# Batched loads for the low halves of w1, a later softmax and an earlier weight request at the change of block size, in a fused convolution and mixture-of-experts kernel

## The chip, the cores and the metric

The kernel runs on one core of one Trainium2 chip. The core has a matrix engine (PE, whose weight loads are listed as PEld), a vector engine (DVE), a scalar engine (ACT), GpSimd (POOL) and SyncE (SP), which here does nothing but issue DMAs. Each engine works through its own list of instructions in order; they wait for one another by semaphores. The metric is the device time in microseconds (us) of one execution; less is better.

## The reference

For 8 sequences of 2880 tokens with 192 features, a causal convolution over 7 tokens is computed with its own softmax weights per token and head (8 heads of 24 features). Its output goes through a mixture of experts: of 4 groups the token takes the best, of that group's 4 experts the best, and its output is the expert's two-layer network times both softmax weights.

```python
w = np.exp(weight_gen - np.max(weight_gen, axis=-1, keepdims=True))
w = w / (np.sum(w, axis=-1, keepdims=True) + 1e-09)
x_unf = x_pad[:, idx, :].reshape(B, S, K, H, group)        # K = 7 taps, 8 heads of 24
x = np.einsum('bshk,bskhg->bshg', w, x_unf).reshape(B * S, D)   # 23040 x 192
g_idx = np.argmax(x @ w_group, axis=1)                     # 4 groups
...
    e_idx = np.argmax(xg @ w_expert[g], axis=1)            # 4 experts in each
    ...
        h = np.maximum(xg[mask_e] @ w1[g, e], 0.0)         # w1: 192 x 1024
        ye = h @ w2[g, e]                                  # w2: 1024 x 192
        out[tok_idx] = combined[:, None] * ye
```

## The kernel before

**Two halves that run side by side.** The *front* takes the tokens in 15 groups of 12 x 128 tokens, two chunks of six to a group. Per group it loads the weights `wt` and the tokens `xin` (`load_group`, L123 and L133), makes the softmax on DVE and ACT (`softmax`: maximum m L269, subtraction L271, exponential on ACT L272, sum z L277 to L281, product L283), forms the seven products per chunk on DVE (L298) and adds them there (L316) or, in the first groups, on PE (L339), computes the routing logits on PE (L379, with the one-hot counts L463) and the choice of expert on DVE (L350 to L493), and lets POOL scatter the tokens by expert into the DRAM table `rows` (L507). A new order of blocks is made whenever a *round* of groups is routed; groups 0 and 1 are the first round, each later one a round of its own.

The *MoE* takes the scattered tokens in blocks. Blocks 0 to 9, those of the first round, are *plain*: one unit of 128 rows, float32 weights as loaded (`wa`, 96x1024 twice), first product `ph` L934, its activation `hh` on ACT, second product `py` L972, output `y` L981. From block 10 on a block has two units of 128 rows and is *split*: its weights `wa` and its tokens are taken apart into a rounded part and a remainder (casts L843 and L852 on ACT, subtraction `wa<-raw,wa` L867 on DVE; tokens `xh` L914 on ACT, `xl` L867 on DVE). For these blocks the remainders of w1's last 64 rows are prepared once, in DRAM, by `halves`.

**halves.** For eight pairs of experts it loads a 128x1024 tile (`fetch`, two DMAs of 64x1024 on SP, L629; the page's DMA part has 256 KB for each), and in `lower_half` casts it with the sign turned (ACT, L621), stores the tile to `w1lo` (SP, L623) and adds the cast one onto it by an accumulating DMA (POOL, L624). The tiles are borrowed from `wa`, `wc` and `raw` buffers, which blocks 0 and on then use.

**What sets the order.** The program's order is made by hand. `front` is a generator that yields after each few instructions, and `blocks` fills it in between the MoE's units by a model of the engines' clocks (`clk`); `Until(t)` holds a generator back until DVE's model clock is t. `side` holds a softmax of the next group, which `beside` advances behind each product of the running group (n counts these steps, 14 to a group). The order that results is then kept on PE, ACT, DVE and SP. Weights are asked for (`ask`, kind 1 and 2 for w1, 3 for w2, 0 for tokens `xb`) by `ask_w` at the last unit of a block, and their DMAs go to SP's list in that order: tables L814, plain w1 L817, split w1 L819 and L826, w2 L830, `xb` L802.

Of the kernel before, what the change touches and what calls it, by code (L numbers as in the profile page):

```python
# [23 lines left out]
AHEAD = (1.0, 1.0, 2.5)  # L24
HURRY = 12
SPACED = range(2, 15)
HALVES = (36.0, 42.0, 48.0, 54.0, 60.0, 66.0, 72.0, 78.0)
WHOLE = 12
SINGLE = tuple((k,) for k in range(7))
MIXED = ((0, 1), (2,), (3,), (4,), (5,), (6,))  # L30
# [12 lines left out]
def conv_moe_kernel(ctx: ExitStack, tc: tile.TileContext, x, wgen, w_group, w_expert, w1, w2, out):  # L43
# [28 lines left out]
    ENDS = [r[0] for r in ROUNDS]  # L72
# [6 lines left out]
    FIRST = ENDS[0]  # L79
# [153 lines left out]
    state = {"slots": False, "open": False, "unit": 0, "starve": False, "ph": 0, "hold": False}  # L233
# [12 lines left out]
    def run(eng, cost, *deps):  # L246
        clk[eng] = max([clk[eng]] + [d + HOP for d in deps]) + cost
        return clk[eng]
# [360 lines left out]
    def halves():  # L609
        spare = wp.tile([P, 3, F], F32, name="wa", bufs=3)  # L610
        raws = [spare[:, k, :] for k in range(3)]
        raws.append(wp.tile([P, NFT, D], F32, name="wc", bufs=4).rearrange("p f d -> p (f d)")[:, 0:F])
        raws += [new_raw[k]() for k in range(2) for _ in range(2)]
        other = wp.tile([P, 3, F], F32, name="wa", bufs=3)
        his = [other[:, k, :] for k in range(3)] + [new_raw[2]()[:, 0:F]]
        his += [wp.tile([P, NFT, D], F32, name="wc", bufs=4).rearrange("p f d -> p (f d)")[:, 0:F] for _ in range(3)]
        his = [t.bitcast(F32R) for t in his]

        def lower_half(k):
            e, hi, raw = 2 * k, his[k % len(his)], raws[k]  # L620
            nc.scalar.activation(out=hi, in_=raw, func=AF.Copy, scale=-1.0)  # L621
            low = w1lo[e:e + 2].rearrange("e p f -> (e p) f")
            nc.sync.dma_start(out=low, in_=raw)  # L623
            nc.gpsimd.dma_start(out=low, in_=hi.bitcast(F32), accum_op=ALU.add)  # L624
            run("pool", 1.1, run("act", 1.0))

        def fetch(k):
            for h in range(2):
                nc.sync.dma_start(out=raws[k][h * HP:(h + 1) * HP, :], in_=w1v[2 * k + h, P:D, :])  # L629

        yield NEXT
        for k, raw in enumerate(raws):
            yield Until(HALVES[k])
            fetch(k)
            if k == 0:
                continue
            lower_half(k - 1)
        yield Until(HALVES[-1] + 6.0)
        lower_half(len(raws) - 1)

    def set_up():
        nc.gpsimd.memset(tri, 1.0)
        nc.gpsimd.affine_select(out=tri, in_=tri, compare_op=ALU.is_gt, fill=0.0, base=0, pattern=[[1, P]], channel_multiplier=-1)
        nc.gpsimd.memset(wr, 0.0)
        wev = w_expert.rearrange("g d e -> d g e")
        for dst, r in ((wr[:, 0, :], slice(0, P)), (wr[0:HP, 1, :], slice(P, D)), (wr[HP:P, 2, :], slice(P, D))):
            nc.gpsimd.dma_start(out=dst[:, 0:G], in_=w_group[r, :])
            nc.gpsimd.dma_start(out=dst[:, G:NL].rearrange("p (g e) -> p g e", g=G), in_=wev[r])
        pad2 = padding()
        for h in range(2):  # L650
            nc.gpsimd.dma_start(out=rows[NROW + h * BK:NROW + (h + 1) * BK, :].rearrange("(p t) c -> p t c", t=2), in_=pad2)
# [4 lines left out]
    def front():  # L656
        side = []
        set_up()
        load_group(1)
        next(slow[0][0])  # L660
        yield from softmax(0, 0, SC)
        rest = softmax(0, SC)

        def pace(g):
            return 99 if g <= FIRST else HURRY if g < MAIN + 3 else 8 if g in ENDS else 2

        def beside(g, n):
            rush = g >= FIRST and not grp[FIRST - 1].routed
            if not rush:
                for q in list(slow):  # L670
                    yield from move(slow, q, 2)
            for q in side[:1]:
                if not rush:
                    yield from move(side, q, 3)
            yield from routing(g)

        def routing(g):
            if ranking:
                yield from move(ranking, ranking[0], pace(g))
            if scoring and (not ranking or g < FIRST):  # L680
                yield from move(scoring, scoring[0], pace(g) if scoring[0][2].chunks == 2 or g >= FIRST - 1 else 3)

        def settle(g):
            while not grp[g].routed:
                qs = ranking or scoring
                q = qs[0]
                yield from move(qs, q, 99)
                if qs and qs[0] is q and q[1] is not None:
                    yield Until(q[1][1]) if q[1][0] == "time" else NEXT

        for g in range(ENDS[-1]):
            o = grp[g]
            o.routed = False
            scoring.append([logits(g, o), None, o])
            for n, c in enumerate(conv(g, o)):
                yield c
                if g == 0 and n < 6:
                    for c in islice(rest, None if n == 5 else 1):
                        yield c
                if n == (2 if state["slots"] else 0) and 1 <= g < ENDS[-1] - 1:  # L700
                    load_group(g + 1)
                if n >= (12 if state["slots"] else 4) and not o.ahead and g + 1 < ENDS[-1] and g != FIRST - 1:
                    o.ahead = True
                    side.append([softmax(g + 1), None])
                yield from beside(g, n)
                if g == FIRST - 1 and n in (7, 8):
                    if n == 7:
                        soft = softmax(FIRST)
                    yield next(soft)
            if g == FIRST - 1:  # L710
                for n, c in enumerate(soft):
                    yield c
                    yield from beside(g, n)
            yield from finish_all(side)
            if g:
                yield from settle(g - 1)
        yield from settle(ENDS[-1] - 1)
# [61 lines left out]
    def plain(n):  # L779
        return order[n][1] == 1  # L780
# [235 lines left out]
    def blocks(n0, n1, paced):  # L1016
# [24 lines left out]
        def ask_w(n):  # L1041
            ask(n, 1)
            ask(n, 2)
# [66 lines left out]
        for i in range(len(units) + LAG):  # L1110
            if i < len(units):
                n, u = units[i]
                last = units_of(n) - 1
                gemm1(cur, u)
                queue.append((cur, u))
                nxt_at = i + last + 1 - u
                if nxt_at < len(units):
                    if u == 0:
                        pump(units[nxt_at][0])
                        nxt = block(nxt_at)  # L1120
                        prep_d(nxt)
                    if u == 1:
                        prep_x(nxt, 0)
                    if u == last // 2 + 1 and nxt.nt > 2:
                        prep_x(nxt, 2)
                if u == last and i + 1 < len(units):
                    cur = nxt
            asks = []
            if i >= LAG:
                b, u = queue.pop(0)  # L1130
                gemm2(b, u)
                if u == units_of(units[i - LAG][0]) - 1:
                    finish(b)
                    if i - LAG + 1 < len(units):
                        asks.append(units[i - LAG][0] + 3)
            if i < len(units):
                n, at = units[i]
                end = at == last
                if end and n + 3 < n1 and (plain(n + 3) or plain(n + 2)):
                    ask_w(n + 3)  # L1140
                    if not plain(n + 3):
                        ask_w(n + 4)
                did = 0
                for job in list(jobs):
                    m, part, h = job
                    if m > n + 2 or (part == 3 and (m > n + 1 or at < LAG)):
                        continue
                    must = end and m == n + 1
                    if not must and (did >= 1 or (m, part) in want or not ready(m)):
                        continue  # L1150
                    jobs.remove(job)
                    work_split(job)
                    did += 1
                state["unit"] += 1
            flush()
            if paced:
                fill(clk["pe"] + AHEAD[0 if cur.plain else 1 if cur.o.whole else 2])
            for a in asks:
                ask_x(a)
            pump()  # L1160
# [45 lines left out]
```

## Time and profile before

| What | us |
|---|---|
| Median of three runs | 1193.74 |
| The three runs | 1194.24, 1193.74, 1187.65 |
| The profiled execution, own time | 1189.24 |
| Its span in the trace | 1187.3 |
| PE busy | 1129.4 (95%) |
| DVE busy | 958.4 (81%) |
| ACT, POOL busy | 647.2 (55%), 580.5 (49%) |

The span runs from the first to the last instruction of the trace; 1.9 us of the execution's own time lie outside it. Busy shares are means over the span. A number in brackets at the end of a row of the timeline is how long the engine stood idle just before, and what ended it; PE's clock in the windows is a share of full speed, 2.4 GHz.

### The profile page before, as it was taken

The numbers are of one execution on the slowest core, as the hardware profiler recorded it, in microseconds if no ns is written. First come the engines' busy times: TensorE is split into PE (matmuls) and PEld (weight loads), VectorE is DVE, ScalarE is ACT, GpSimd is POOL, SyncE is SP. The second block draws the span as 40 slices with busy tenths as digits, with TensorE's granted clock in tenths as the row PEclk, the third lists the DMA queues.
The fourth block names the chain that finished last, engine by engine and source line by source line (L and its number), as shares of the span: only waits on it lengthen the run. The fifth ranks groups of instructions, "written<-read, shape, count | busy, mean of one in ns | idle before, by whom it ended". The sixth has DMA issues, their size and how long they took to land.

```text
span 1187.3 us, 24563 instructions
## 1 busy us (share of the span) xinstructions
PE 1129.4 (95%) x8357; PEld 1070.3 (90%) x8357; DVE 958.4 (81%) x1666; ACT 647.2 (55%) x1235; POOL 580.5 (49%) x611
## 2 busy tenths in 40 slices
PE   5787899999999999999999999999999989999998
PEld 3444789999999999999999999999899989999997
DVE  8899898999998999999999999998554756556661
ACT  1331344655556556556555556555556756666572
POOL 7154173848175756566555747373766112222211
PEclk9997999999999999999999999999999989999999
DMA  5797799896878877978787878667788775665562
GB/s 173 217 306 221 250 298 286 251 294 216 290 233 280 257 259 215 302 222 287 222 293 219 298 212 277 193 200 233 224 258 263 217 200 140 177 171 177 165 203 73
DMA packets 83880, 275.10 MB, mean 232 GB/s; under 512 B 15357, under 2 KB 33732, under 8 KB 81952
## 3 DMA queue, kind: packets, MB, share of 16 engines
q1 hardware_dynamic: 63416, 229.77, 62.6%
q0 software_dynamic: 20208, 43.39, 12.0%
q8 instruction: 67, 1.10, 0.4%
q14 instruction: 69, 0.57, 0.2%
q10 hardware_dynamic: 120, 0.28, 0.1%
HBM read 225.83 MB, written 48.42 MB: 231 GB/s over the span
## 4 chain that ended last, share of the span: by engine, by line
PE 73%; DVE 9%; issue 7%; DMA 5%; ACT 3%; POOL 2%; SPq 1%; POOLq 0%; ACTq 0%; DVEq 0%
PE ph L934 31%; PE py L972 27%; PE py L974 3%; DVE pr L298 3%; PE pl L379 2%; PE tpx L908 2%; PE py L975 1%; PE tpx L909 1%; POOL out L989 1%; DMA raw<-in_moe_w 1%; DMA wt<-in_weight_gen 1%; PE ph L339 1%; DMA rows<-xrow,posi 1%; PE pl L974 1%; PE tp L396 1%
## 5 line engine op out<-in xcount | busy, mean ns | idle before, releaser
L934 PE MATMUL ph<-xh,wa 128*128 128x256 f32 (+2 forms) x1992 | 459.9, 305 | 0.0
L989 POOL DMA_INDIRECT out<-y,xb x189 | 207.8, 1100 | 420.3 <-DVE y L987 188.9
L972 PE MATMUL py<-wc,hh 128*128 128x192 f32 x2160 | 400.4, 327 | 2.0 <-ACT y L981 2.0
L934 PE MATMUL ph<-xl,wa 128*128 128x256 f32 (+2 forms) x1328 | 355.9, 287 | 0.0
L972 PEld LDWEIGHTS py<-wc,hh 128*128 128x128 f32 x2160 | 346.1, 190 | 2.4 <-ACT y L981 2.2
L934 PEld LDWEIGHTS ph<-xh,wa 128*128 128x128 f32 x1992 | 336.9, 190 | 3.3 <-issue 1.8
L940 ACT ACTIVATE hh<-ph 128x512 f32<-128x512 f32 (+2 forms) x296 | 165.6, 559 | 261.4 <-PE ph L934 261.2
L298 DVE TENSOR_TENSOR pr<-xin,wt 128x1152 f32<-128x1152 f32 x186 | 249.2, 1352 | 5.9 <-PE py L339 3.7
L507 POOL DMA_INDIRECT rows<-xrow,ix x156 | 227.5, 1458 | 48.2 <-POOL ix L506 35.8
L934 PEld LDWEIGHTS ph<-xl,wa 128*128 128x128 f32 x1328 | 250.7, 189 | 0.0
L316 DVE TENSOR_TENSOR xrow<-xrow,pr 128x1152 f32<-128x1152 f32 x144 | 194.8, 1353 | 0.7
L867 DVE SCALAR_TENSOR_TENSOR pr<-ph,hh 128x320 fp32r<-128x320 f32 (+2 forms) x128 | 73.9, 578 | 98.3 <-ACT hh L945 97.5
L867 DVE TENSOR_TENSOR wa<-raw,wa 128x1024 fp32r<-128x1024 f32 x83 | 101.5, 1223 | 29.1 <-ACT wa L843 20.8
L974 PE MATMUL py<-wc,hh 128*128 128x384 f32 x352 | 113.3, 369 | 0.0
L506 POOL COPY ix<-posi 128x1 int32<-128x1 int32 x156 | 77.0, 504 | 70.2 <-DMA rows<-xrow,ix 42.4
L945 ACT ACTIVATE hh<-ph 128x320 fp32r<-128x320 f32 (+2 forms) x128 | 65.4, 511 | 66.6 <-PE ph L934 66.2
L975 PE MATMUL py<-wc,pr 128*128 128x192 f32 x352 | 88.9, 253 | 0.0
L843 ACT CAST wa<-raw 128x1024 fp32r<-128x1024 f32 x83 | 87.1, 1050 | 3.0 <-DMA raw<-w1lo 3.0
L852 ACT CAST wa<-raw 128x1024 fp32r<-128x1024 f32 x83 | 86.7, 1044 | 0.7 <-DMA raw<-w1lo 0.7
L981 ACT ACTIVATE y<-py,xb 128x192 f32<-128x192 f32 x179 | 67.2, 422 | 21.4 <-PE py L972 19.7
L867 DVE TENSOR_TENSOR xl<-tpx,xh 128x512 fp32r<-128x512 f32 (+1 forms) x94 | 60.7, 646 | 15.5 <-ACT xh L914 15.0
L974 PEld LDWEIGHTS py<-wc,hh 128*128 128x128 f32 x352 | 67.2, 191 | 1.3
(187 smaller groups left out, 1354.3 us busy)
## 6 DMA issues: line engine op xcount, KB each, us to landing
wc<-in_moe_w SPq DMA_DIRECT2D x73, 768.0 KB
raw<-in_moe_w SPq DMA_DIRECT2D x83, 512.0 KB
xin<-in_x SPq DMA_DIRECT2D x14, 1728.0 KB
raw<-in_moe_w SPq DMA_DIRECT2D x91, 256.0 KB
raw<-w1lo SPq DMA_DIRECT2D x83, 256.0 KB
raw<-in_moe_w SPq DMA_DIRECT2D x22, 768.0 KB
xb<-rows SPq DMA_DIRECT2D x79, 194.0 KB
wa<-in_moe_w SPq DMA_DIRECT2D x24, 384.0 KB
```

The costliest lines, as they stand in the source:

```text
L298: nc.vector.tensor_tensor(out=dst, in0=o.xin[:, c0 + k:c0 + k + SC, :].rearrange("p s (h g) -> p s h g", g=HG), in1=w4[:, c0:c0 + SC, :, k ...
L316: nc.vector.tensor_tensor(out=acc, in0=acc, in1=prs[k - 2], op=ALU.add)
L507: written_once(nc.gpsimd.indirect_dma_start(out=rows[:, :], out_offset=bass.IndirectOffsetOnAxis(ap=ix, axis=0), in_=src, in_offset=None, ...
L843: nc.scalar.copy(out=o.wa[:, 0, :], in_=o.raw[0])
L852: nc.scalar.copy(out=o.wa[:, 2, :], in_=o.raw[1])
L867: f(*a, **k)
L934: nc.tensor.matmul(ph[:, v, :], lhsT=w[:, f0:f0 + P], rhs=rhs, start=i == 0, stop=i == len(terms) - 1)
L940: nc.scalar.activation(out=hh, in_=ph, func=AF.Relu)
L972: nc.tensor.matmul(b.acc[t], lhsT=hh[:, v, c], rhs=wc[0][:, f, :], start=f == 0 and not (b.wide and t == 1), stop=f == NFT - 1 and not (b. ...
L974: nc.tensor.matmul(b.py[t], lhsT=hh[:, v, c], rhs=wc[f // 4][:, f % 4].rearrange("p l d -> p (l d)"), start=f == 0, stop=False)
L975: nc.tensor.matmul(b.acc[t], lhsT=hl[:, v, c], rhs=wc[f // 4][:, f % 4, 0, :], start=False, stop=f == NFT - 1)
L989: ins = nc.gpsimd.indirect_dma_start(out=out[:, :], out_offset=bass.IndirectOffsetOnAxis(ap=b.x.bitcast(I32)[:, t, D + 1:D + 2], axis=0), ...
```

## The change

Three things are changed. `halves` issues all sixteen loads in one batch, at model time 20, beside group 0's convolution; the eight lower halves follow one by one from 29 to 72. The next group's softmax starts behind step 12, not 4, for the groups after `FIRST` (2), which touches the softmaxes of groups 4 and 5 (later ones stand behind step 12 already). And at the change from plain to split blocks the weights of block 10 are asked for at the end of block 6, ahead of block 9's, those of block 11 alone at the end of block 7, where before both 10 and 11 were asked for at the end of block 7.

```diff
@@ -24,7 +24,8 @@
 AHEAD = (1.0, 1.0, 2.5)
 HURRY = 12
 SPACED = range(2, 15)
-HALVES = (36.0, 42.0, 48.0, 54.0, 60.0, 66.0, 72.0, 78.0)
+FETCH = 20.0
+HALVES = (29.0, 34.0, 39.0, 45.0, 51.0, 58.0, 65.0, 72.0)
 WHOLE = 12
 SINGLE = tuple((k,) for k in range(7))
 MIXED = ((0, 1), (2,), (3,), (4,), (5,), (6,))
@@ -629,14 +630,12 @@
                 nc.sync.dma_start(out=raws[k][h * HP:(h + 1) * HP, :], in_=w1v[2 * k + h, P:D, :])
 
         yield NEXT
-        for k, raw in enumerate(raws):
+        yield Until(FETCH)
+        for k in range(len(raws)):
+            fetch(k)
+        for k in range(len(raws)):
             yield Until(HALVES[k])
-            fetch(k)
-            if k == 0:
-                continue
-            lower_half(k - 1)
-        yield Until(HALVES[-1] + 6.0)
-        lower_half(len(raws) - 1)
+            lower_half(k)
 
     def set_up():
         nc.gpsimd.memset(tri, 1.0)
@@ -699,7 +698,7 @@
                         yield c
                 if n == (2 if state["slots"] else 0) and 1 <= g < ENDS[-1] - 1:
                     load_group(g + 1)
-                if n >= (12 if state["slots"] else 4) and not o.ahead and g + 1 < ENDS[-1] and g != FIRST - 1:
+                if n >= (12 if state["slots"] or g > FIRST else 4) and not o.ahead and g + 1 < ENDS[-1] and g != FIRST - 1:
                     o.ahead = True
                     side.append([softmax(g + 1), None])
                 yield from beside(g, n)
@@ -1136,10 +1135,13 @@
             if i < len(units):
                 n, at = units[i]
                 end = at == last
-                if end and n + 3 < n1 and (plain(n + 3) or plain(n + 2)):
+                if end and n + 4 < n1 and plain(n + 3) and not plain(n + 4):
+                    ask_w(n + 4)
                     ask_w(n + 3)
-                    if not plain(n + 3):
-                        ask_w(n + 4)
+                elif end and n + 3 < n1 and plain(n + 3):
+                    ask_w(n + 3)
+                elif end and n + 4 < n1 and plain(n + 2):
+                    ask_w(n + 4)
                 did = 0
                 for job in list(jobs):
                     m, part, h = job
```

SP's list at the start, from the loads of group 1 on; `w1lo<-` are the stores, wt and xin the loads of groups 2 and 3. Before:

```order
L133 DMA xin<-in_x 128x3456
L629 DMA wa<-in_moe_w 64x1024 x2
L623 DMA w1lo<-wa 128x1024
L629 DMA wa<-in_moe_w 64x1024 x2
L623 DMA w1lo<-wa 128x1024
L629 DMA wc<-in_moe_w 64x1024 x2
L623 DMA w1lo<-wa 128x1024
L629 DMA raw_194<-in_moe_w 64x1024 x2
L623 DMA w1lo<-wc 128x1024
L629 DMA raw_193<-in_moe_w 64x1024 x2
L623 DMA w1lo<-raw_194 128x1024
L629 DMA raw_196<-in_moe_w 64x1024 x2
```

And now:

```order
L630 DMA wa<-in_moe_w 64x1024 x6
L630 DMA wc<-in_moe_w 64x1024 x2
L630 DMA raw_194<-in_moe_w 64x1024 x2
L630 DMA raw_193<-in_moe_w 64x1024 x2
L630 DMA raw_196<-in_moe_w 64x1024 x2
L630 DMA raw_195<-in_moe_w 64x1024 x2
L624 DMA w1lo<-wa 128x1024 x3
L124 DMA wt<-in_weight_gen 128x672
L134 DMA xin<-in_x 128x3456
L624 DMA w1lo<-wc 128x1024
L624 DMA w1lo<-raw_194 128x1024
L624 DMA w1lo<-raw_193 128x1024
```

The sixteen loads stand in a row ahead of all stores, three stores are ahead of group 2's wt and xin, and the last store is ahead of group 3's, where it stood behind the weights of blocks 0 and 1.

SP's list at the change of block size (tab holds a round's list of experts; raw_193 and raw_195 are block 10's w1, wa and xb_173 block 9's). Before:

```order
L817 ISA
L817 DMA wa<-in_moe_w 96x1024
L800 TENSOR_LOAD tab_818
L800 ISA x2
L802 ISA
L802 DMA xb_173<-rows 128x194
L830 ISA
L830 DMA wc<-in_moe_w 128x1536
L814 TENSOR_LOAD tab_1372
L814 ISA x2
L819 ISA
L819 DMA raw_193<-in_moe_w 128x1024
```

And now:

```order
L818 ISA
L818 DMA raw_193<-in_moe_w 128x1024
L825 ISA
L825 DMA raw_195<-in_moe_w 64x1024
L825 ISA
L825 DMA raw_195<-w1lo 64x1024
L813 TENSOR_LOAD tab_821
L813 ISA x2
L816 ISA
L816 DMA wa<-in_moe_w 96x1024
L816 ISA
L816 DMA wa<-in_moe_w 96x1024
```

Block 10's three loads come ahead of block 9's wa and xb, right behind block 8's wc.

DVE's list in group 3's first chunk, with group 4's softmax (m and z of wt) and group 2's routing (mxg and on). Before:

```order
L298 TENSOR_TENSOR pr<-xin,wt 128x1152
L269 TENSOR_REDUCE m<-wt 128x96
L271 TENSOR_TENSOR wt<-wt,m 128x672
L316 TENSOR_TENSOR xrow<-xrow,pr 128x6x192
L298 TENSOR_TENSOR pr<-xin,wt 128x1152
L316 TENSOR_TENSOR xrow<-xrow,pr 128x6x192
L298 TENSOR_TENSOR pr<-xin,wt 128x1152
L316 TENSOR_TENSOR xrow<-xrow,pr 128x6x192
L277 TENSOR_REDUCE z<-wt 128x96
L279 TENSOR_SCALAR z<-z 128x96
L281 RECIPROCAL z<-z 128x96
L350 TENSOR_REDUCE mxg<-ls 128x12
```

And now, from the end of group 2's routing on (the chunk's other products and sums stand ahead of it; the lines here are one higher):

```order
L354 TENSOR_TENSOR le<-le,mxe 128x48
L359 SCALAR_TENSOR_TENSOR dfe<-le,j_116 128x48
L362 TENSOR_REDUCE ixe<-dfe 128x12
L365 TENSOR_TENSOR ohe<-dfe,ixe 128x48
L317 TENSOR_TENSOR xrow<-xrow,pr 128x6x192
L270 TENSOR_REDUCE m<-wt 128x96
L272 TENSOR_TENSOR wt<-wt,m 128x672
L449 TENSOR_TENSOR ohs<-ohe,sgn 128x48
L451 TENSOR_REDUCE smg<-exg 128x12
L454 TENSOR_TENSOR oh<-ohg,ohs 128x192
```

Group 4's m and subtraction now come behind the routing's ohe and are all that stands of that softmax ahead of oh; z and the product follow later.

## Rows read from the trace of the kernel before

**Rows 1.** The page, part 1: busy us, share of the span, instructions.
```profile
PE 1129.4 (95%) x8357; PEld 1070.3 (90%) x8357; DVE 958.4 (81%) x1666; ACT 647.2 (55%) x1235; POOL 580.5 (49%) x611
```

**Rows 2.** Windows: stretch, length, busy by engine, PE clock, DMA share, GB/s.
```profile
20.00:40.00 20.00, 17.51 (x73) 10.12 (x72) 18.07 (x18) 3.39 (x7) 3.09 (x6) 1.00 0.19 60
...
160.00:200.00 40.00, 35.91 (x289) 34.34 (x288) 33.78 (x68) 14.99 (x38) 21.50 (x24) 0.91 0.94 283
200.00:400.00 200.00, 196.48 (x1552) 192.90 (x1551) 186.67 (x299) 116.44 (x218) 118.05 (x109) 1.00 0.84 259
400.00:600.00 200.00, 200.00 (x1587) 197.62 (x1586) 185.75 (x293) 120.53 (x224) 126.84 (x117) 1.00 0.80 253
```

**Rows 3.** Timeline of DVE, 126 to 177: start, us, line, idle before.
```profile
126.48 0.85 DVE L269 TENSOR_REDUCE m<-wt 128x96 f32<-128x672 f32 x1 [3.69 <-DMA wt<-in_weight_gen]
...
133.22 1.35 DVE L316 TENSOR_TENSOR xrow<-xrow,pr 128x1152 f32<-128x1152 f32 x1
134.49 0.84 DVE L277 TENSOR_REDUCE z<-wt 128x96 f32<-128x672 f32 x1
...
136.28 0.14 DVE L350 TENSOR_REDUCE mxg<-ls 128x12 f32<-128x48 f32 x1
...
140.69 0.85 DVE L283 TENSOR_TENSOR wt<-wt,z 128x672 f32<-128x672 f32 x1
...
176.32 0.85 DVE L269 TENSOR_REDUCE m<-wt 128x96 f32<-128x672 f32 x1 [2.51 <-DMA wt<-in_weight_gen]
```

**Rows 4.** Timeline of PE, 142 to 201, same columns.
```profile
142.10 0.24 PE L463 MATMUL pl<-oh,tri 128*128 128x192 bf16 x1 [2.10 <-DVE oh L453]
...
194.78 0.92 PE L972 MATMUL py<-wc,hh 128*128 128x192 f32 x4 [2.01 <-ACT y L981]
195.53 1.77 PE L934 MATMUL ph<-xd,wa 96*128 96x128 f32 x8
...
199.61 0.82 PE L972 MATMUL py<-wc,hh 128*128 128x192 f32 x4
200.27 1.06 PE L934 MATMUL ph<-xd,wa 96*128 96x128 f32 x8
201.16 0.28 PE L908 MATMUL tpx<-ident,xb 128*128 128x128 f32 x1
```

**Rows 5.** Timeline of SP: DMA issues from 118 to 186.
```profile
118.70 0.86 SPq L817 DMA_DIRECT2D wa<-in_moe_w  x2
...
171.04 0.57 SPq L830 DMA_DIRECT2D wc<-in_moe_w  x1
181.12 0.86 SPq L817 DMA_DIRECT2D wa<-in_moe_w  x2
...
185.69 0.33 SPq L819 DMA_DIRECT2D raw<-in_moe_w  x1
```

**Rows 6.** The chain that ended last, 121 to 193: start, us, what.
```profile
121.39 5.06 DMA wt<-in_weight_gen
...
168.82 7.47 DMA wt<-in_weight_gen
...
185.69 6.95 DMA raw<-in_moe_w
```

**Rows 7.** Timeline of ACT, 192 to 195.
```profile
192.82 1.04 ACT L843 CAST wa<-raw 128x1024 fp32r<-128x1024 f32 x1 [3.03 <-DMA raw<-w1lo]
...
194.30 0.42 ACT L981 ACTIVATE y<-py,xb 128x192 f32<-128x192 f32 x1
```

**Rows 8.** Timeline of DVE: the xl of blocks 10 and 13.
```profile
203.27 0.68 DVE L867 TENSOR_TENSOR xl<-tpx,xh 128x512 fp32r<-128x512 f32 x1
...
231.75 0.69 DVE L867 TENSOR_TENSOR xl<-tpx,xh 128x512 fp32r<-128x512 f32 x1 [0.49 <-ACT xh L914]
```

**Rows 9.** Timeline of PE: first matmuls of blocks 10 and 13.
```profile
205.39 0.54 PE L934 MATMUL ph<-xh,wa 128*128 128x256 f32 x2
...
241.63 0.53 PE L934 MATMUL ph<-xh,wa 128*128 128x256 f32 x2
```

## The prediction

> **What bounds the kernel now.** I read the page's busy times first: PE is at work in 1129.4 of 1187.3 us [rows 1], so 58 us at most can be won from its gaps, and a change like this one, which takes no work off PE, can only win there. The windows say where the gaps lie. From 400 to 600 PE is busy in all 200 us, from 200 to 400 in 196.48, and DVE in about 186 of each 200, so that it too is nearly full; from 160 to 200 PE lacks 4.1 us and DVE 6.2 [rows 2]. Before about 110 the first groups run at DVE's pace, and PE waits for it (17.51 of 20 us between 20 and 40, DVE 18.07 [rows 2]). So I looked one by one at the places before 210 where PE waits once the MoE has begun, and for each at what it waits for, back to a DMA.
>
> Two are to be seen. At 142.10 PE waits 2.10 us for the one-hot oh of group 2's routing [rows 4]. DVE made oh late because it stood 3.69 us waiting for group 4's wt [rows 3], which SP issued at 121.39 and which took 5.06 us to land [rows 6]. At 194.78 PE waits 2.01 us for y [rows 4], which ACT made at 194.30, behind a cast at 192.82 that had waited 3.03 us for a raw tile of block 10 [rows 7]. That tile's first DMA went out at 185.69 and took 6.95 us [rows 6]. A third wait, 2.51 us of DVE for group 5's wt [rows 3], shows no wait of PE behind it. The change has its hand on all three.
>
> **The batch of loads.** It adds no work: sixteen DMAs, eight casts, stores and accumulates, as before. What moves is when. The sixteen loads are 256 KB each, 4 MB. They go out from about 9 us on, and between 20 and 40 the DMA engines are busy to 0.19 at 60 GB/s, where 283 GB/s stand in 160 to 200 [rows 2]. At the difference of the two, 223 GB/s, 4 MB take 19 us, so my estimate is that they are through by about 30, before group 2's wt and xin would be wanted. Those have three stores ahead of them on SP, which want only the first three pairs, 1.5 MB or 7 us by the same rate: there by 20, no delay. ACT's casts, 1.04 each by the nearest like row [rows 7], eight of them, fall where ACT is busy in 3.39 of 20 us [rows 2]: nothing, and if that cover were gone, a cast's length each. POOL's accumulates move ahead of the scatters of group 1, where POOL is idle; if one of them stood in the scatters' way it would cost about a us, as a POOL DMA there does.
>
> What comes of it is that the last store and accumulate are out of the way of block 2's weights, which at 118.70 [rows 5] had to wait for the accumulate; SP then reaches group 4's wt some us earlier, 3 at most by my estimate, since 118.70 to 121.39 is what SP needs from that point. So the batch alone would shorten the wait of 3.69, perhaps take it all.
>
> **The later softmax.** By the order DVE no longer meets m of group 4 in the middle of the chunk. Ahead of oh there were ten products and sums, the whole softmax and a wait of 3.69; now there are twelve, and of the softmax only m and the subtraction. The sum from rows: minus 3.69, minus 1.79 for the z steps (134.49 to 136.28), minus 0.85 for the product at 140.69, plus 2 x 1.27 (133.22 to 134.49) [rows 3]: minus 3.8, so oh comes 3.8 us earlier, where 2.1 are enough for PE. **Minus 2.1 us on PE.** The two edits meet here and each would do most of it; their gains do not add. Group 5's softmax goes the same way, past its 2.51, off PE's path: 0 there.
>
> **Block 10's weights.** Asked at the end of block 6 they go out right behind block 8's wc, issued at 171.04 [rows 5], instead of 185.69: 14 us earlier. At 7 us to land, or 10 in a bad case, they are there by 181, and the cast wants them at about 189.8 (192.82 less 3.03 [rows 7]). Block 9's wa is now queued behind them on SP; it went out at 181.12 after SP had stood idle, waiting for a wa buffer [rows 5], so the three DMA issues ahead of it, a few us, fit between 171 and 181: 0. So the wait of 2.01 goes. Behind it PE ran slowly: the two pairs of ph and py from 194.78 to 199.61 took 4.83 us, where a pair at full pace takes 1.55 (199.61 to 201.16 [rows 4]), so 3.10: 1.73 more. The windows show the granted clock at 0.91 in that stretch [rows 2]. I take that this goes with the wait: **minus 3.7 us.** Were the slow pairs there for another reason, it is minus 2.0.
>
> The start of the MoE waits on the scatters and xb of group 1; with 4 MB moved away from 40 to 100 these could land sooner, with the stores moved to nearby they could not. I take 0.2, between 0 and 3. **Sum: -2.1 - 3.7 - 0.2 = -6.0 us.**
>
> **What is late next.** PE would arrive 6 us sooner in a stretch where DVE has little to spare. Block 10's xl begins at 203.27 and is 0.60 long, PE's first product with it starts at 205.39: 1.5 spare. Block 13's begins at 231.75 and PE wants it at 241.63: 9.3 spare [rows 8, 9]. Between these two xl the order has four more products and sums (5.1 us) and six softmax steps (0.85 + 0.87 + 1.79 + 0.85, 4.3 us) more than before, since the work that DVE did earlier and the softmax come here: 9.4 us. If DVE, like PE, moves forward by 6, nothing of the 9.3 is left. DVE loses more waits than PE does, though: 3.69 and 2.51, and 1.6 to 2.8 behind casts at blocks 10 and 11, up to 10. So the margin at block 13 is between 0 and 4, and I give back 1 us of the 6: **-5 net**, with ends at -9 and at +3.
>
> Against the execution profiled, 1189.24, that is 1184; against the median, 1193.74, it is 1189. The three runs span 1187.65 to 1194.24 and the profiled one is near their low end, so I take the middle, **1186.5**.
>
> **The rule on queues.** The rows show group 1's loads issued just ahead of the batch, and no row shows what a batch does to them. The Trainium skill, "DMA: Bandwidth & Descriptors", section "Queues, rings and completion order", says that in one queue of an engine descriptors start in order, and that an engine goes round between queues by packets. By that rule group 1's loads keep their place ahead of the 4 MB, and only what is issued behind it waits; at the page's mean of some 436 GB/s the batch would be an estimated 9.6 us, not 19, and the sum would not move. No run here shows it yet.
>
> **The rivals.** *DVE becomes the bound after block 10.* For it: 186 busy of 200 from 200 on [rows 2], and the margin of 0 to 4 above. Then PE waits at the start of blocks 12 to 14 for 2 to 5 us in all and the gain is 0 to 3: 1188 to 1193. *The same, but repeated, and slower in the end.* Should DVE come late at each block's start, every stop costs its wait and the slow pairs behind it, 2.01 + 1.73 = 3.7 [rows 4]. One or two stops eat the gain; from the third on the kernel loses, and four would give +15 - 6, about +9: 1203, six about 1210. The point from which it decides is DVE's total: it has 13 us free in each 200. Against it: DVE's work is the same in sum, so only the shift of 9.4 can make it late, once. *The batch stands in the way of the first stage.* DVE needs group 1's wt early and any us that it waits there is a us of the front. All that SP has asked for by then, with the batch some 6.6 MB, at 283 GB/s is 23 us; loads shared evenly could come 7 us late, less the 6 won: 1194 to 1196. Against it is that they are issued first. *More than I count:* the xb of block 0 sooner by up to 3, the other gaps before 200 (4.1 us in 160 to 200 [rows 2]) closing as well: -12, 1178 to 1181. *It does nothing of this:* the waits are replaced by others of their length, 1193.
>
> **How the numbers follow.** A change of 1%, 12 us, is about what a measurement of this kernel can tell from none. Chances: the forecast, gain 3 to 8, 0.50 (1183 to 1190); DVE the bound or nothing gained, 0.27 (1188 to 1194); the batch in the way, 0.06 (1194 to 1196); more than counted, 0.12, of which most passes the 12 us only when the median stays at its high end; repeated stops, 0.05 (1200 to 1210). The range 1177 to 1195 leaves out the last, some of the batch's case and half of the largest gain. Faster by over 1%: 0.11. Slower by over 1%: 0.05. Within: 0.84.
>
> **What would show it.** In the changed kernel's timeline: m of group 4 and 5 without a wait for wt; L463 at about 136 to 140 without a wait; no wait of ACT for raw at block 10 and no slow pairs behind y; block 10 on PE some 6 us earlier than 205.39; loads of `halves` all issued by 20 and group 2's wt still at 37. Wrong I would be if PE shows new waits for xl at blocks 11 to 14, if DVE waits for wt or xin before 40, or if from 200 on PE falls behind what it did before.

## The result: 0.8% slower, and the profile after

The changed kernel takes 1202.33 us (median of six runs, 1200.85 to 1203.83), the kernel before in the same comparison 1189.46. The ratio is 1.0076, with a 95% interval of 1.0051 to 1.0100. The forecast was 1186.5, a gain; the time lies above the range's end of 1195. The profiled execution took 1200.85 us, its span is 1199.2, which is 11.9 more than the span of before.

PE's work is the same; what grew is the time in which it stands or runs slowly. The page's part 1 after:

```profile
PE 1126.8 (94%) x8357; PEld 1068.2 (89%) x8357; DVE 957.3 (80%) x1666; ACT 647.1 (54%) x1235; POOL 568.7 (47%) x611
```

The windows after, with the same columns as [rows 2], the stretch from 200 on cut finer:

```profile
20.00:40.00 20.00, 14.53 (x58) 8.03 (x57) 16.14 (x15) 5.54 (x10) 4.97 (x8) 0.83 0.99 261
...
160.00:200.00 40.00, 34.46 (x298) 32.69 (x297) 34.29 (x70) 15.18 (x39) 25.73 (x26) 1.00 0.96 307
200.00:250.00 50.00, 43.77 (x346) 41.54 (x346) 44.11 (x55) 27.36 (x52) 25.66 (x25) 0.97 0.90 281
...
600.00:800.00 200.00, 194.08 (x1506) 191.16 (x1505) 176.01 (x302) 113.44 (x214) 119.21 (x117) 0.98 0.76 246
```
Two of the same stretches before, which [rows 2] doesn't show by themselves:

```profile
200.00:250.00 50.00, 48.35 (x394) 46.95 (x393) 46.47 (x62) 30.62 (x59) 32.45 (x28) 1.00 0.92 278
...
600.00:800.00 200.00, 200.00 (x1602) 197.15 (x1601) 185.21 (x312) 117.57 (x222) 116.37 (x114) 1.00 0.76 244
```
The first groups are slower (20 to 40: 14.53 us of PE's work instead of 17.51, DMA engines full at 0.99 instead of 0.19), 200 to 250 has 4.6 us less of it, and 600 to 800, where PE had not stood still at all, 5.9 less, at 0.98 of full clock. From 160 to 200 PE is busy 1.5 us less, but at full clock, where before it had 0.91 of it.

Where the time goes is best seen on the blocks. The table gives the start of each block's first product on PE (block 0: its first ph; from block 10 on the first with xl), changed kernel less before, each from the two timelines, in us.

| Block | 0 | 10 | 11 | 12 | 13 | 14 | 16 | 30 | 60 | 61 | 70 | 80 | 92 |
|---|---|---|---|---|---|---|---|---|---|---|---|---|---|
| later by | +3.3 | -1.3 | +1.8 | +1.8 | +4.9 | +4.9 | +4.2 | +4.2 | +4.3 | +13.7 | +13.1 | +11.8 | +11.9 |

So block 0 is late, block 10 is early by less than forecast, two steps of 3.1 follow at blocks 11 and 13, and one of 9.4 at block 61, some 550 us behind the last place that the change touches. These four places are read in turn.

**The first chunk.** The chain that ended last, after, has two DMAs in its first 200 us that the chain before does not have (start, us, what). The second belongs to block 10:

```profile
22.68 9.04 DMA rows<-rem
...
193.26 6.11 DMA xb<-rows
```
The first is the write of the padding rows (what a block without tokens reads) from the tile `rem`; POOL issues it at 22.07. Its 9.04 us end at 31.7, and ACT, which fills the same tile for the first chunk's transposes, waits for it; PE waits for ACT (ACT's row, then PE's):

```profile
31.82 0.51 ACT L390 COPY rem<-xrow 128x384 f32<-128x384 f32 x1 [3.93 <-DMA rows<-rem]
```
```profile
32.38 0.47 PE L398 MATMUL tp<-ident,rem 128*128 128x128 f32 x1 [4.80 <-ACT rem L390]
```
Most of the 9.04 us is not the write itself. POOL's queue (`software_dynamic`) has six small loads of the routing weights `wr` ahead of the padding rows. Its packets, MB and share of the DMA engines before, from 19 to 23 us and from 23 to 25, and then after, from 23 to 27.6 and from 27.6 to 31:

```profile
q0 software_dynamic: 192, 0.02, 13.4%
...
q0 software_dynamic: 128, 0.40, 60.7%
```
```profile
q0 software_dynamic: 192, 0.02, 5.8%
...
q0 software_dynamic: 128, 0.40, 35.1%
```
From 19 to 23 this queue moved nothing in the changed kernel. So the small loads came through 4 to 5 us late beside the batch, and the padding rows behind them took 3 us instead of 2.

**Blocks 0 to 10.** The waits that the change was to remove are gone. On DVE neither m waits for wt any more (compare [rows 3]):

```profile
139.34 0.85 DVE L270 TENSOR_REDUCE m<-wt 128x96 f32<-128x672 f32 x1
...
141.23 0.36 DVE L454 TENSOR_TENSOR oh<-ohg,ohs 128x192 bf16<-128x192 f32 x1
...
202.52 0.84 DVE L270 TENSOR_REDUCE m<-wt 128x96 f32<-128x672 f32 x1
```
PE's wait for group 2's oh is gone (141.86), and so is that for y behind block 10's raw tile (compare [rows 4]). In its place two waits for tokens stand on PE's timeline, 2.15 us for block 9's and 1.17 for block 10's, and one for ACT's copy behind them:

```profile
141.86 0.25 PE L464 MATMUL pl<-oh,tri 128*128 128x192 bf16 x1
...
191.64 0.42 PE L898 MATMUL tp<-ident,xb 128*96 128x128 f32 x2 [2.15 <-DMA xb<-rows]
...
199.41 0.33 PE L907 MATMUL tpx<-ident,xb 128*128 128x128 f32 x1 [1.17 <-DMA xb<-rows]
...
204.04 0.53 PE L933 MATMUL ph<-xh,wa 128*128 128x256 f32 x2
...
211.91 0.33 PE L398 MATMUL tp<-ident,rem 128*128 128x128 f32 x1 [2.82 <-ACT rem L390]
```
SP's timeline shows why. Block 10's weights go out at 172.27, as forecast, and block 9's wa at 179.61, sooner than before. Then SP stands for 7.5 us, until 188.81, because block 9's tokens are to go into a buffer that an earlier block's output scatter still reads. Block 10's tokens come behind that and behind block 11's weights:

```profile
172.27 0.34 SPq L818 DMA_DIRECT2D raw<-in_moe_w  x1
...
179.61 0.88 SPq L816 DMA_DIRECT2D wa<-in_moe_w  x2
188.81 0.36 SPq L801 DMA_DIRECT2D xb<-rows  x1
...
190.67 0.34 SPq L818 DMA_DIRECT2D raw<-in_moe_w  x1
...
193.26 0.35 SPq L801 DMA_DIRECT2D xb<-rows  x1
```
**Blocks 10 to 13.** The wait of 2.82 us at 211.91 is for the first chunk of group 4. On PE's list its transposes now stand behind the second step of block 10's ph, where before they stood behind the fourth. ACT's list has not come to the copy by then: from 207.5 to 211.3 ACT works without a gap at casts and copies of the MoE and at the exponential of group 5's softmax. A wait of 1.64 at 235.94, for the second chunk, is of the same kind. Behind it the granted clock is 0.50 from 238 to 241, and the 48 short products of the logits (L380) take 2.8 us, where before they took 1.5 at full clock.

**Block 61.** PE waits 5.86 us for tokens and is at half clock behind (eight py take 2.77 us at 782.60 and 1.47 at 787.94). PE's rows, and then the window from 781.5 to 785.5 with the columns of [rows 2]:

```profile
781.36 0.48 PE L907 MATMUL tpx<-ident,xb 128*128 128x128 f32 x1 [5.86 <-DMA xb<-rows]
...
782.60 2.77 PE L971 MATMUL py<-wc,hh 128*128 128x192 f32 x8
...
787.94 1.47 PE L971 MATMUL py<-wc,hh 128*128 128x192 f32 x8
```
```profile
781.50:785.50 4.00, 3.93 (x14) 3.55 (x15) 2.54 (x3) 3.17 (x7) 1.13 (x3) 0.50 1.03 380
```
The chain that ended last leads, from 740 to 800, back to POOL: an output scatter at 774.05, which frees the buffer, and the load into it at 777.55:

```profile
774.05 3.29 DMA out<-y,xb
777.55 3.77 DMA xb<-rows
```
POOL's timeline before, and then after, at this place (start, us, line, idle before):

```profile
762.70 0.97 POOL L989 DMA_INDIRECT out<-y,xb  x1 [7.38 <-ACT y L981]
763.97 0.97 POOL L989 DMA_INDIRECT out<-y,xb  x1 [0.30 <-ACT wa L852]
...
765.96 0.98 POOL L507 DMA_INDIRECT rows<-xrow,ix  x1 [0.15 <-POOL ix L506]
```
```profile
765.48 0.98 POOL L508 DMA_INDIRECT rows<-xrow,ix  x1 [0.15 <-POOL ix L507]
...
771.63 1.80 POOL L508 DMA_INDIRECT rows<-xrow,ix  x1 [0.28 <-POOL ix L507]
...
774.05 1.92 POOL L988 DMA_INDIRECT out<-y,xb  x1 [0.15 <-issue]
776.28 0.97 POOL L508 DMA_INDIRECT rows<-xrow,ix  x1 [0.30 <-issue]
777.55 0.97 POOL L988 DMA_INDIRECT out<-y,xb  x1 [0.30 <-issue]
```
Before, the two scatters of an earlier block's output went out at 762.70 and 763.97, ahead of group 12's scatters into `rows`. After, five of group 12's stand ahead of the first of them and another ahead of the second. SP waits for them (its queue's waits from 735 to 800, before and after: us in all, times, longest):

```profile
SPq L802 <- DMA out<-y,xb: 14.3, 2, 10.2
```
```profile
SPq L801 <- DMA out<-y,xb: 24.2, 2, 17.5
```

### The profile page after: what moved, and what is told of

Its sections match the earlier page's. It is cut to its first block, busy times and chain, and to the rows that moved or that the text cites. A ratio compares the mean times of both kernels' runs of the same rounds, so it can differ in the third digit from the quotient of the medians.

```text
span 1199.2 us, 24547 instructions
## 1 busy us (share of the span) xinstructions
PE 1126.8 (94%) x8357; PEld 1068.2 (89%) x8357; DVE 957.3 (80%) x1666; ACT 647.1 (54%) x1235; POOL 568.7 (47%) x611
## 3 DMA queue, kind: packets, MB, share of 16 engines
q0 software_dynamic: 20208, 43.39, 11.8%
## 4 chain that ended last, share of the span: by engine, by line
PE 67%; issue 17%; POOL 5%; DVE 4%; DMA 3%; ACT 2%; POOLq 0%; SPq 0%; DVEq 0%; ACTq 0%
PE ph L933 28%; PE py L971 27%; POOL out L988 3%; PE pl L380 2%; DVE pr L299 2%; PE tpx L908 1%; PE ph L340 1%; PE tpx L907 1%; PE py L973 1%; DMA xb<-rows 1%; DMA raw<-w1lo 1%; DMA rows<-rem 1%; PE pl L397 1%; PE tp L397 1%; PE py L340 1%
## 5 line engine op out<-in xcount | busy, mean ns | idle before, releaser
L988 POOL DMA_INDIRECT out<-y,xb x189 | 220.0, 1164 | 441.8 <-DVE y L986 185.9
L508 POOL DMA_INDIRECT rows<-xrow,ix x156 | 216.0, 1385 | 48.2 <-POOL ix L507 35.0
L507 POOL COPY ix<-posi 128x1 int32<-128x1 int32 x156 | 65.4, 429 | 70.9 <-DMA rows<-xrow,ix 40.2
```

What stands on the lines that cost most here:

```text
L508: written_once(nc.gpsimd.indirect_dma_start(out=rows[:, :], out_offset=bass.IndirectOffsetOnAxis(ap=ix, axis=0), in_=src, in_offset=None, ...
L988: ins = nc.gpsimd.indirect_dma_start(out=out[:, :], out_offset=bass.IndirectOffsetOnAxis(ap=b.x.bitcast(I32)[:, t, D + 1:D + 2], axis=0), ...
```

## The experiments

The first four ran on one chip, on which the kernel before took 1192.04 us; runs five to eight and nine to eleven on two others, on which it took 1224.38 and 1221.45. So each is given as a ratio to the kernel before on its own chip. Starts of blocks are compared with the trace of before. The chips of the last seven lose time in each later group whatever the kernel (last section), so these are compared only up to block 14, and at block 13 with care: the fifth, tenth and eleventh run, which leave group 5's softmax as it was, lose 2.5 to 5.4 us there too, where the first and third run lose nothing.

**First run: the batch alone.** The change's part in `halves`:

```diff
-        for k, raw in enumerate(raws):
-            yield Until(HALVES[k])
-            fetch(k)
...
+        yield Until(FETCH)
+        for k in range(len(raws)):
+            fetch(k)
```

> The batch of loads alone; softmax and weight requests as in the kernel before. Theory A (most of the loss comes from POOL's list, which the later softmax changes): POOL's list of scatters is that of before, so block 61 starts without a stall; the first groups are 3.8 us late as in the changed kernel, since ACT waits for the padding rows, but DVE's wait of 3.69 for group 4's wt takes that up; time within 3 us of before. Rival B (the batch itself makes the loss, as the padding rows are written 4 us later and everything behind is late): 4 us slower or more, up to the whole 12. The prediction's step (the batch alone shortens the wait for wt and gains about 2): 2 faster.

Measured: ratio 0.9984 (0.9959 to 1.0010). So there is no loss, and rival B falls; a gain of 2 us lies inside the interval. Block 0 is 2.9 us late, block 10 1.8, block 61 3.1, and there is no stall at block 61. DVE's wait for group 4's wt, now 1.21 us, took most of the lateness up, as theory A has it. PE's wait for oh is shorter by 1.2 us (0.89), but the wait behind block 10's raw tile is there still, and longer by 1.8:

```profile
195.66 1.65 PE L971 MATMUL py<-wc,hh 128*128 128x192 f32 x4 [3.77 <-ACT y L980]
```
**Second run: the later softmax alone.**

```diff
-                if n >= (12 if state["slots"] else 4) and not o.ahead ...
+                if n >= (12 if state["slots"] or g > FIRST else 4) and not o.ahead ...
```

> The later softmax alone. Theory A: POOL's list has five of group 12's scatters into rows ahead of the two scatters of an earlier block's output, as in the changed kernel, the tokens of block 61 come some 10 us late, PE waits about 6 us and runs slowly behind it, so 8 to 9 us are lost there; at the wait for the one-hot 2 us are won; time 5 to 9 slower than before. Rival B (batch): no loss without the batch, 0 to 2 faster. The prediction's step: 2 faster.

Measured: ratio 1.0079 (1.0054 to 1.0104): the whole loss, without the batch. Block 10 is 0.5 early, block 11 3.0 late, block 13 6.2, block 60 5.5, block 61 13.6. The wait for oh is gone, but the one behind block 10's raw tile has grown from 2.01 to 5.21 us: SP issues that tile at 184.97, hardly sooner than before (185.69). So the 2 us won at oh are lost again there. PE's timeline has this wait, those for ACT's copies and the one at block 61 (two stretches of one timeline):

```profile
193.79 1.65 PE L972 MATMUL py<-wc,hh 128*128 128x192 f32 x4 [5.21 <-ACT y L981]
...
211.69 0.33 PE L397 MATMUL tp<-ident,rem 128*128 128x128 f32 x1 [2.14 <-ACT rem L389]
...
237.18 0.33 PE L397 MATMUL pl<-ident,rem 128*128 128x128 f32 x1 [1.64 <-ACT rem L389]
```
```profile
782.49 0.47 PE L908 MATMUL tpx<-ident,xb 128*128 128x128 f32 x1 [5.76 <-DMA xb<-rows]
```
**Third run: the early weights alone.**

```diff
+                if end and n + 4 < n1 and plain(n + 3) and not plain(n + 4):
+                    ask_w(n + 4)
+                    ask_w(n + 3)
```

> Block 10's weights asked for one block earlier, alone. The prediction's step: the wait of 2.0 for the cast and the slow pairs behind it go, 3.7 faster. Theory C (the tokens xb of block 10 land at about 200.7 in any case, since they are asked for behind block 9's xb and block 11's weights): the wait goes but PE stands as long for xb a few us later; within 1.5 us of before. POOL's list is that of before, so no stall at block 61 in either case.

Measured: ratio 0.9979 (0.9955 to 1.0004), some 2.5 us faster, between theory C's 1.5 and the prediction's 3.7; the interval holds both. The trace speaks for theory C: block 10 is no earlier. The wait for y is gone, and on PE stand these instead, for block 9's and block 10's tokens:

```profile
191.73 0.42 PE L899 MATMUL tp<-ident,xb 128*96 128x128 f32 x2 [1.36 <-DMA xb<-rows]
...
201.04 0.33 PE L908 MATMUL tpx<-ident,xb 128*128 128x128 f32 x1 [2.28 <-DMA xb<-rows]
```
Block 10 starts 1.7 us later than before in this trace, though its block 0 was 2.1 earlier.

**Fourth run: the change with POOL's order mended at group 12.** Pinned to the order in which they are written, one unit later:

```diff
+        if g in (12,):
+            yield NEXT
         for s in range(n):
             run("pool", 2.2 if g in SPACED else 1.28, clk["dve"])
...
+            if r == 11:
+                tc.keep_in_program_order(ins)
```

(the copies of the indices are pinned in the same way).

> The whole change, but group 12's scatters into rows are put on POOL behind the two output scatters that they stood ahead of; group 12's choice of expert moves by one unit for it, all else as in the changed kernel. Theory A: the wait of 5.9 us for block 61's tokens goes, and the clock stays up behind it; block 61 is as late as block 60, some 4 us instead of 13; 8 to 9 us faster than the changed kernel, 2 to 5 slower than before. Rival B (the loss is the front's, and block 61 only shows it): the stall stays, or comes a block later; no faster than the changed kernel by more than 2.

Measured: ratio 1.0049 (1.0026 to 1.0071). POOL's timeline has the two output scatters ahead again:

```profile
768.16 1.34 POOL L995 DMA_INDIRECT out<-y,xb  x1 [6.58 <-ACT y L987]
769.81 0.98 POOL L995 DMA_INDIRECT out<-y,xb  x1 [0.31 <-ACT hh L946]
...
771.26 0.98 POOL L512 DMA_INDIRECT rows<-xrow,ix  x1 [0.28 <-POOL ix L509]
```
SP loads the tokens at 771.00 instead of 777.55, and block 61 is 5.9 us late where block 60 is 5.5: the step of 9.4 is gone. The medians of the second and the fourth run, 1201.87 and 1196.50 on one chip, say 5.4 us, the spans of their traces, 1200.7 and 1192.6, 8.1. The 8 to 9 expected are not reached in the medians; in the trace 1.0 us is lost at block 64, and blocks 11 to 13 lose 1.2 more than in the changed kernel's trace. Rival B falls: the stall is POOL's order. What is left is the loss at blocks 11 and 13, which lasts: block 60 is 5.5 late and block 92 5.0.

**Fifth and sixth run: the later softmax of group 4 alone, and of group 5 alone** (`g == 3` and `g == 4` in place of the second run's `g > FIRST`).

> The later softmax for group 4 alone, all else as before. Theory A (narrowed: it is group 5's softmax that shifts POOL's list and loads ACT between blocks 10 and 13): POOL's list from group 3 on is that of before, no stall at block 61, no lag between blocks 10 and 13; the wait of 2.1 for the one-hot goes; 0 to 3 us faster than before. Rival D (either softmax does the harm): 4 us slower or more.

> The later softmax for group 5 alone, all else as before. Theory A: the whole loss: 5 to 7 us between blocks 10 and 13, where PE waits for ACT's copies of group 4's first chunk, 8 to 9 us at block 61; 9 to 13 slower than before. Rival D: half of it.

Measured: 0.9991 (0.9958 to 1.0023) and 1.0124 (1.0051 to 1.0198, of four executions). The harm is group 5's: POOL's list is that of before from group 3 on in the fifth run, and has the two output scatters behind group 12's in the sixth. The sixth has the waits for ACT's copies and a step of 9.5 us from block 60 to block 61; the fifth has neither. The sixth's waits:

```profile
215.73 0.33 PE L397 MATMUL tp<-ident,rem 128*128 128x128 f32 x1 [2.82 <-ACT rem L389]
...
241.44 0.33 PE L397 MATMUL pl<-ident,rem 128*128 128x128 f32 x1 [1.64 <-ACT rem L389]
```
The fifth run's gain of up to 3 us was not found, and its timeline shows why, as the second run's does. The wait for oh is gone, and the one behind block 10's raw tile, issued at 188.16, is longer instead:

```profile
197.77 1.65 PE L972 MATMUL py<-wc,hh 128*128 128x192 f32 x4 [6.04 <-ACT y L981]
```

**Seventh run: block 10's tokens ahead of block 11's weights**, on top of the third run.

```diff
                 elif end and n + 4 < n1 and plain(n + 2):
-                    ask_w(n + 4)
+                    behind.append(n + 4)
...
             for a in asks:
                 ask_x(a)
+                while behind:
+                    ask_w(behind.pop())
```

> Block 10's weights asked for early as in the third run, and block 11's weights put behind block 10's tokens in SP's list. Theory C (block 10 waits for its tokens, which land late as their DMA stands behind block 9's tokens and block 11's weights): the tokens are asked for some 2 us earlier and without 1 MB ahead of them, the wait of 2.3 at block 10 goes, block 10 starts 3 us earlier than in the third run; 1 to 4 faster than before. If only the landing of block 3's output scatter holds them, nothing is won: within 1.5 of the third run.

Measured: 0.9958 (0.9928 to 0.9988), some 5 us of 1224, a little more than expected. Its profiled execution took 1239.74 us, far above its other runs, so its waits are not read here.

**Eighth run: the change, with the padding rows in another tile,** the one that block 0's tokens take later.

```diff
-        pad2 = padding()
+        pad = xbs[0][:, 0, :]
+        nc.gpsimd.memset(pad, 0.0)
+        nc.gpsimd.memset(pad.bitcast(I32)[:, W - 1:W], PADID)
+        pad2 = pad.unsqueeze(1).broadcast_to([P, 2, W])
```

> The whole change, but the padding rows are written from a tile of their own (the tokens' tile of block 0), so that ACT's copy need not wait until they are written. Theory A: the wait of 4.8 us at the first chunk goes, the first groups run as before to 0.3 us and block 0 starts at 115.5 instead of 119; at the end little of it is left, as block 10 waits for its tokens anyway and block 61 for its own: 0 to 2 faster than the changed kernel. Rival B: 4 us or more faster.

Measured: 1.0036 (0.9991 to 1.0082); the medians, 1233.46 and 1224.38, give 1.0074. The wait of 4.8 is gone. Block 0 starts at 115.05 and block 10 4.5 us earlier than before; block 13 is 2.8 late again. PE's timeline has the waits that the padding rows have nothing to do with:

```profile
189.17 0.42 PE L901 MATMUL tp<-ident,xb 128*96 128x128 f32 x2 [2.02 <-DMA xb<-rows]
...
208.80 0.48 PE L398 MATMUL tp<-ident,rem 128*128 128x128 f32 x1 [2.82 <-ACT rem L390]
```
Against the changed kernel's 1.0076, on another chip, that is some 5 us by the ratio and nothing by the medians, so the time settles nothing. The trace says 3.2 at block 10 (-4.5 instead of -1.3). So the front's delay did cost something there, more than the 0 to 2 that theory A gave it; whether it lasts to the end isn't shown, and rival B's 4 can't be excluded.

**Ninth run: fourth and eighth together.**

> The whole change, with group 12's scatters put behind the two output scatters (fourth run) and the padding rows in a tile of their own (eighth run). If the three places found are all there is, what is left is the loss between blocks 10 and 13, some 7 us, less the 4 to 5 by which block 10 starts earlier: block 10 at -4 to -5 against before, block 14 at +2 to +3, the end at +1 to +3; 0 to 3 us slower than before. If something else is lost after block 14, 5 slower or more.

Measured: 0.9953 (0.9926 to 0.9980), 5 to 6 us faster than before, where at best no difference was expected. Block 10 is 3.5 early and block 14 4.1 late, with the two waits of 2.82 and 1.64; expected were 4 to 5 early and 2 to 3 late. Where the gain comes from isn't shown: there is no trace of before on that chip.

**Tenth and eleventh run: the batch, own padding rows, early weights and tokens,** without the later softmax and with group 4's.

> The batch with the padding rows in a tile of their own, block 10's weights asked for early, block 11's behind block 10's tokens; softmax as before. Block 10 starts 3 to 5 us earlier than before, nothing is lost between blocks 10 and 13 nor at block 61; 2 to 5 us faster than before. If the prediction's rival of DVE as the bound behind block 10 holds, PE waits for xl at blocks 11 to 14 and 2 or less are left.

> The same with group 4's softmax behind step 12 as well, group 5's as before. The one-hot of group 2 is 2 us earlier than in the tenth run, POOL's list behind group 3 is that of before: 4 to 7 us faster than before. If block 10 still waits for its tokens, as in the third run, the 2 us are lost there and the time is that of the tenth run.

Measured: 0.9946 (0.9922 to 0.9971) and 0.9959 (0.9933 to 0.9985). Both beat the kernel before on their chip, by 6.6 and 5.0 us; the changed kernel was not run there. Group 4's later softmax adds nothing that can be measured, though block 10 is 4.1 early with it and 2.4 without. PE waits for no xl at blocks 11 to 14 in either trace. That nothing is lost between blocks 10 and 13 was not met: 5.4 and 2.7 us are lost at block 13, where PE waits 3.94 and 1.97 us for ACT's copy of the logits.

## Why the prediction was wrong

The step that failed is *"What is late next"*: it asked only for DVE and its xl and gave back 1 us. Three stops came instead, at blocks 11, 13 and 61, of 3.1, 3.1 and 9.4 us, and none of them is for xl. The first two are for ACT's copies, the third is for tokens that POOL's changed order held back, and for POOL the sum had put nothing but one accumulate. By its steps:

- *The batch, "no delay", 0.* Half right. Group 2's wt was in time (issued at 40.62, not at 37, but DVE's m at 56.03 doesn't wait for it), and so were the casts. The loads were issued until 27.5, not 20, and the one of 23.06 landed at 32.6, so "through by about 30" was a few us short. What failed is that only SP's own queue was counted. The write of the padding rows stands in POOL's queue behind six small loads, and ACT's `rem` hung on it. The cost at block 0 was 3.3 us, and it is gone in the eighth run. In the batch alone 2.5 of 2.9 us came back out of DVE's wait.
- *The later softmax, -2.1 at oh.* Right in kind: the wait went. The sum of -3.8 on DVE was right as well: DVE was 3.3 us late when it entered the chunk (122.18 instead of 118.89), and oh came 0.46 us earlier than before. What failed is adding the 2.1 to the 3.7. In the second and the fifth run PE gave the gain back at the next wait, for block 10's raw tile, which was issued at most 0.7 us sooner than before.
- *Block 10's weights, -3.7.* The wait and the slow pairs went. The first DMA took 14.2 us to land, not 7 to 10, and was still in time. But "and the wait of 2.01 goes" was taken as a gain of PE, without asking what else block 10 needs. Its tokens landed only at 199.4 (193.26 and 6.11). The third run shows the same term by itself: the waits for tokens, 1.36 and 2.28, are together as long as the wait of 2.01 and the 1.73 of slow pairs. It was to be seen before, in an ACT row that waited for these tokens:

```profile
200.74 0.41 ACT L892 COPY xd<-xb 128x256 f32<-128x256 f32 x1 [0.48 <-DMA xb<-rows]
```
- *"What is late next", DVE and its xl.* After block 10, PE's timeline has no wait for xl over 0.15 us before 970, and there the old one has it too (3.58, and 3.64 before). What came late were the tokens, through POOL's output scatters, and ACT's copies. A small misreading changes nothing: xl of block 10 takes 0.68 us, not 0.60, and 205.39 is a product with xh; the first with xl starts at 205.76, so 1.8 was spare, not 1.5. Of the prediction's signs of being wrong, the last, PE behind from 200 on, came true; xl and DVE's loads show nothing new.
- *POOL.* The order of the kernel is kept on PE, ACT, DVE and SP; POOL's is not, and it changed in groups 2, 3, 4, 6, 8, 10, 12 and 13. From block 16 to block 60 the block starts keep their distance from before within 0.5 us, though groups 4, 6, 8 and 10 are reordered there; only group 12's change made a stop. The step at block 61, 9.4 of 11.9 us, is wholly POOL's order: absent where group 12's scatters stand as before (first, third, fifth, tenth run), present where they don't (second, sixth, eighth), gone when that order is mended (fourth, ninth).
- *ACT's copies.* The sum has no term for them. That they go with group 5's later softmax is shown by the fifth and the sixth run; that it is PE's order ahead of ACT's is read from the two lists, and no run mends that order alone.
- *The rivals.* "It does nothing of this: the waits are replaced by others of their length" is what the third run shows for the weights. *The rival of repeated stops* gave 1203, nearly the time measured, but by luck: it had four stops of 3.7 for DVE's xl, and there were three, of 3.1, 3.1 and 9.4, in other places and of other causes. Its kind of price, a wait with a slow stretch behind it, holds for the last two. The rival of the batch in the first stage's way was right in that the stage came late, but by the padding rows and not by group 1's wt, which DVE has at 15.85 (before 15.77) without a wait.

**The rule on queues** was weighed for SP's loads alone. By the Trainium skill, "DMA: Bandwidth & Descriptors", section "Queues, rings and completion order", an engine goes round between queues by packets, so that a small DMA of another queue need not wait for all of a batch. The trace agrees in part: from 23 to 31 both queues move packets, but from 19 to 23 POOL's queue moved none beside SP's 0.98 MB, and no run here says why. The 436 GB/s of the prediction, which that page of the Trainium skill has as the rate of a fit and not as a mean, was not reached: 0.98 MB in 4 us are 245 GB/s, near the 223 of the sum.

What stays open: why the ninth run is 5 us faster than before, with 4.1 lost at block 14, and what the eighth run's tile is worth at the end. On the eighth run's chip the fifth run's trace is the nearest to one of before (ratio 0.9991); against it the eighth run is 3.4 us early at block 14, 5.1 early at block 60 and 3.1 late at block 61. So part of what it lost at block 13 against the trace of before may be the chip's, which isn't shown.

## What to carry to other kernels

Ask of every engine whose order the program doesn't fix whether its list changes, down to the end of the kernel: a change in one group can put two instructions in another order 550 us later. When a wait on the path goes, list everything that the next step needs, with the time at which each lands; the wait is worth the gap to the second latest. Before adding up two waits on one engine, ask whether what the second one waits for comes sooner too; if not, the first gain is lost there. A batch that fits into idle bandwidth can still delay the small DMAs of another queue beside it, and whoever shares a buffer with them.

## Of the hardware, not expected

The kernel before has medians of 1189.46 and 1192.04 in two comparisons, and of 1224.38 and 1221.45 on two other chips, 2.5 to 2.9% more. In the fifth run's trace, on one of these, the loss against the trace of before grows in steps of 3 to 5 us, one to a group, from 8.6 at block 24 to 33.7 at block 60. In some of these groups PE stands ahead of the logits' short products (L379) 0.2 to 0.8 us at a time without anything that the profile shows, and in some 0.8 to 2.6 us for ACT's copy of their result. What makes it is not known; it is why later blocks were not compared across chips.
